# The scores of every attention unit as one float32 product of q and k as loaded, instead of three products of split operands

## The chip, the cores and the metric

The kernel runs on one core of a Trainium2 chip. The metric is the device time of one execution in microseconds (us). Lower is better.

## The reference

Two stages follow each other: an attention with a memory term, and a two-layer network on its output. B, H, S, D are 4, 8, 576, 64.

```python
scores = scale * np.matmul(q, k.transpose(0, 1, 3, 2))
scores = np.where(causal, -1000000000.0, scores)
a = softmax(scores)                       # max subtracted, sum + 1e-09
local = np.matmul(a, v)
q_p = np.where(q > 0, q, np.exp(q) - 1.0) + 1.0
mem_out = einsum(q_p, M_prev) / (einsum(q_p, z_prev)[..., None] + 1e-06)
g = sigmoid(beta)
x = (g * mem_out + (1 - g) * local)       # transposed to 2304 tokens x 512
h = x @ w_in                              # 512 -> 2048
out = (np.maximum(h, 0) ** 2) @ w_out     # 2048 -> 512
```

## The kernel before

The attention is cut into units (b, p, tiles): one batch b, one pair p of heads, and some of the four query tiles 1 to 4 of 128 tokens each (tile 0, the first 64 tokens of all batches, is done at the start by `first_tokens`). Units 0 to 3 are batch 0 with tiles 1 and 2, units 4 to 7 batch 0 with tiles 3 and 4, units 8 to 11 and 12 to 15 the same for batch 1, and units 16 to 23 are batches 2 and 3 with all four tiles. Within a unit the tiles run in the order `TORD` = 2, 1, 3, 4. The keys of tiles 2, 1, 3 are 320, 192, 448 wide, and tile 4 has two groups of 288. The two heads of a pair lie on partitions 0 to 63 and 64 to 127, and their products (`sp`) run beside each other.

A unit does this. `loads` issues, on SyncE's queue (SP), k as `kd`, then q together with the memory as `qm` (of which `q_raw` is the q part), and v as `vv`. `kd` has one buffer (`KB` = 1), `qm` two, `vv` one. The loads of the next unit are issued from `after()`, ahead of the unit's tiles. Of units 6 to 23 (`sfull` false) q and k are split into a high part (`qh`, `kh`, rounded to fp32r on ScalarE) and the rest (`ql`, `kl`, a subtraction on VectorE, in some units GpSimd), and the scores are the sum of three fp32r products. Of units 0 to 5 (`NES` = 6) they are one float32 product of `q_raw` and `kd`. Then come the mask and row maximum (`mx`, VectorE), `e` = exp (ScalarE), the split of e into two f16 halves `a` (L514 on ScalarE, L516 on VectorE), a DMA transpose `aT` on SP's queue, the products with v (`acc`), and the sum with the memory term in `memx`, which goes to DRAM (`xd`) for every two tiles.

The network (`moe`) runs in nine blocks of 256 tokens. A block starts by reading its tokens back (`xn`), transposing them on TensorE (`px`) and splitting them (`xh`, `xl`). Then it has 192 products `up` (L624 to L626) and 96 products `oacc` (L614 to L616). Block 0 is the first tokens, block 1 is batch 0 with tiles 1 and 2 (units 0 to 3), block 2 batch 0 with tiles 3 and 4 (units 4 to 7), and so on. `px` of block 2 therefore needs all of units 4 to 7.

The kernel is written in a framework whose scheduler fixes the order of the instructions on each engine from its own model of the times, and places the waits; each engine then runs its list in order. The names of the steps are those of the code.

Of the kernel before, what the change touches and what calls it, by code (L numbers as in the profile page):

```python
# [8 lines left out]
F32 = mybir.dt.float32  # L9
F32R = mybir.dt.float32r  # L10
# [11 lines left out]
P = 128  # L22
# [6 lines left out]
SQ = S - D  # L29
# [4 lines left out]
SC = 16384.0  # L34
VEXP = 14
VL = 'dd'
PM = 'pd'
FX = 'dd'
GHN = 4
VMIN = 2.0**-80  # L40
NEF = 2
NES = 6
PXT = 'up'
PXE = 'aa'
PHI = 1
QB = 2
VVB = 1
ZW = D + 1
# [2 lines left out]
EB = 3  # L51
# [3 lines left out]
PJ = 6  # L55
SEQ = 'a0 b0 g a1 r b1 r c0 l r r c1'
W0 = 9
EARLY = 'dp'
LATE = 'dd'
NEARLY = 12  # L60
SEG = 2
TORD = [2, 1, 3, 4]
# [25 lines left out]
def fused_kernel(ctx: ExitStack, tc: tile.TileContext, t0_d, zt_d, kk_d, qv_d, beta, w_in, w_out, out):  # L88
    nc = tc.nc
# [3 lines left out]
    at = ctx.enter_context(tc.tile_pool(name="at", bufs=1))  # L93
# [13 lines left out]
        out=mask, in_=mask, pattern=[[-1, MW]], compare_op=ALU.is_ge, fill=-1e30, base=448, channel_multiplier=1  # L107
# [219 lines left out]
    dp = ctx.enter_context(tc.tile_pool(name="dp", bufs=1, space=bass.MemoryType.DRAM))  # L327
# [12 lines left out]
        nc.sync.dma_start(vv[:, :nv], qv_d[b, p, :, SQ + 2 * ZW : SQ + 2 * ZW + nv])  # L340
        return kd, qm, vv

    def attention(b, p, tiles, ld, after, early, sfull, full):
        q_eng, k_eng = (nc.gpsimd if c == 'p' else nc.vector for c in (EARLY if early else LATE))
        late = 0 if early else 1
        h0 = 2 * p
        tl = tiles[-1]
        kn, ncn = sum(QT[tl]), tl + 1
        qa, qb = QT[tiles[0]][0] - D, kn - D
        kd, qm, vv = ld  # L350
        q_raw = qm[:, 2 * ZW :]
        mz = qm[:, : 2 * ZW]
        v = vv.rearrange("p (c x) -> p c x", c=5)
        heads = [slice(h * D, (h + 1) * D) for h in range(2)]

        if not sfull:
            qh, ql = (at.tile([P, SQ], F32R, tag=t, name=t) for t in ("qh", "ql"))
            kh, kl = (at.tile([P, S], F32R, tag=t, name=t) for t in ("kh", "kl"))
            nc.scalar.copy(qh[:, qa:qb], q_raw[:, qa:qb])
            q_eng.tensor_tensor(  # L360
                out=ql[:, qa:qb], in0=q_raw[:, qa:qb], in1=qh[:, qa:qb].bitcast(F32), op=ALU.subtract
            )
            yield
            nc.scalar.copy(kh[:, :kn], kd[:, :kn])
            k_eng.tensor_tensor(out=kl[:, :kn], in0=kd[:, :kn], in1=kh[:, :kn].bitcast(F32), op=ALU.subtract)
            yield
            terms = [(qh, kh), (ql, kh), (qh, kl)]
        else:
            terms = [(q_raw, kd)]

        pe = at.tile([P, 2, S], F32, tag="e", name="pe", bufs=EB)[:, 0]
        w = slice(qa, qb)
        nc.scalar.activation(pe[:, w], q_raw[:, w], AF.Exp)
        ph = pe if sfull else q_raw
        if PHI and not sfull:
            nc.scalar.activation(q_raw[:, w], q_raw[:, w], AF.Relu)
            nc.vector.scalar_tensor_tensor(
                out=q_raw[:, w], in0=pe[:, w], scalar=1.0, in1=q_raw[:, w], op0=ALU.min, op1=ALU.add
            )
        else:  # L380
            m_eng = nc.gpsimd if PM[late] == "p" else nc.vector
            m_eng.tensor_scalar(out=pe[:, w], in0=pe[:, w], scalar1=1.0, scalar2=None, op0=ALU.min)
            nc.vector.scalar_tensor_tensor(
                out=ph[:, w], in0=q_raw[:, w], scalar=0.0, in1=pe[:, w], op0=ALU.max, op1=ALU.add
            )
        yield

        if not full:
# [11 lines left out]
                out=vy, in0=vy, scalar1=VMIN, scalar2=2.0**-VEXP, op0=ALU.max, op1=ALU.mult  # L400
# [19 lines left out]
        for grp in (tiles[:2], tiles[2:]):  # L420
# [4 lines left out]
            for j, i in enumerate(grp):  # L425
# [6 lines left out]
                out=nm[:, :ng], in0=pv[:, :, :, D], scalar=1e-6,  # L432
# [6 lines left out]
                in0=pv[:, :, :, :D],  # L439
# [7 lines left out]
        for i in [t for t in TORD if t in tiles]:  # L447
# [8 lines left out]
            for s in range(ns):  # L456
                ks = slice(s * w, (s + 1) * w)
                sps = ps.tile([P, 2, 512], F32, tag="s", name="sp")
                for x, (qt, kt) in enumerate(terms):
                    for h, hd in enumerate(heads):  # L460
                        nc.tensor.matmul(  # L461
                            sps[:n, h, :w], qt[hd, qc], kt[hd, ks], start=x == 0, stop=x == len(terms) - 1
                        )
                for h in range(2):
                    nc.vector.tensor_tensor_reduce(  # L465
                        out=e[:n, h, ks],
                        in0=sps[:n, h, :w],
                        in1=mask[:n, 448 - q0 + s * w : 448 - q0 + s * w + w],
                        scale=-0.125,
                        scalar=3e38 if s == 0 else mx[:n, h, 0:1],  # L470
                        op0=ALU.add,
                        op1=ALU.min,
                        accum_out=mx[:n, h, s : s + 1],
                    )
# [229 lines left out]
    def attn(i0, i1):  # L704
        for i in range(i0, i1):
            ld = nxt.pop()

            def after():
                if i + 1 < len(order):
                    nxt.append(loads(*order[i + 1]))  # L710

            yield from attention(*order[i], ld, after, i < NEARLY, i < NES, i < NEF and max(order[i][2]) < 4)

    def na(t):
        return NP * (6 + (len(t) > 3) + 2 * len(t) - 1)
# [64 lines left out]
```

## Time and profile before

| what | value |
|---|---|
| median of 3 runs | 610.11 us (610.11 to 610.82) |
| the profiled execution's own time | 609.23 us |
| its span, first to last instruction | 607.4 us |
| TensorE (PE) busy | 569.1 us, 94% of the span |
| VectorE (DVE), ScalarE (ACT), GpSimd (POOL) busy | 411.2, 329.0, 170.3 us |
| mean granted TensorE clock | 0.986 of full speed |

PE is the matmul stream, PEld its weight loads, which overlap it. A line such as L461 is a line of the kernel before. The last scores are computed at about 478 us; after that only the network is left.

### The profile page before, as it was taken

The page shows a single profiled execution, that of the slowest core. Times are in us where ns is not written, and L with a number is a line of the kernel's source. Part 1 is how long each engine was busy: PE and PEld are TensorE (multiplying, and loading weights), DVE is VectorE, ACT ScalarE, POOL GpSimd, SP SyncE. Part 2 cuts the span into 40 slices and gives each one's busy share as a digit, 9 for nine tenths or more (in the row PEclk, how much of TensorE's full clock was granted, in tenths as well). Part 3 has the DMA queues.
Part 4 walks back from the last instruction along what each step waited for, and adds up shares of the span by engine and source line. Part 5 has one row for each costly group of instructions (what it writes and reads, how often), then busy time and mean ns, then how long its engine had stood idle before and what let it go on. Part 6 is the DMA issues. An engine that isn't in the chain of part 4 may idle for free.

```text
span 607.4 us, 11542 instructions
## 1 busy us (share of the span) xinstructions
PE 569.1 (94%) x4198; PEld 482.7 (79%) x4198; DVE 411.2 (68%) x1285; ACT 329.0 (54%) x747; POOL 170.3 (28%) x139
## 2 busy tenths in 40 slices
PE   2479997999989999999999999999999999999997
PEld 2358876787868787888888888888888899998996
DVE  5999798868677879887888978788697711001000
ACT  3689686756566664775576645654556413312312
POOL 2501232134423233233332233232321121221221
PEclk9989998999997999999999999999999999999999
DMA  8947575673574775664655564575435510100000
GB/s 278 402 144 301 165 210 159 139 169 85 117 165 111 160 155 129 145 173 88 164 115 114 145 126 107 114 167 118 103 70 119 99 24 2 68 1 1 36 1 35
DMA packets 127576, 76.28 MB, mean 126 GB/s; under 512 B 99360, under 2 KB 112672, under 8 KB 127520
## 3 DMA queue, kind: packets, MB, share of 16 engines
q1 hardware_dynamic: 127520, 75.55, 49.7%
q8 instruction: 33, 0.54, 0.4%
q14 instruction: 23, 0.19, 0.1%
HBM read 42.63 MB, written 8.78 MB: 85 GB/s over the span
## 4 chain that ended last, share of the span: by engine, by line
PE 63%; DVE 13%; DMA 9%; ACT 9%; issue 3%; SPq 1%; POOL 1%; ACTq 0%
PE up L624 9%; PE up L626 8%; PE up L625 8%; PE oacc L614 8%; PE oacc L616 8%; PE oacc L615 8%; PE sp L461 6%; DMA aT<-a 3%; DMA vv<-in_qv_dram 3%; ACT e L477 2%; PE acc L546 2%; DVE a L516 2%; PE pm L428 2%; DVE e L465 2%; DVE memx L556 2%
## 5 line engine op out<-in xcount | busy, mean ns | idle before, releaser
L624 PE MATMUL up<-xh,w 128*128 128x256 f32 x576 | 167.0, 290 | 3.4 <-ACT aF L496 2.5
L626 PE MATMUL up<-xh,w 128*128 128x256 f32 x576 | 166.1, 288 | 0.0
L625 PE MATMUL up<-xl,w 128*128 128x256 f32 x576 | 165.9, 288 | 0.0
L639 POOL TENSOR_TENSOR gl<-r,gh 128x512 fp32r<-128x512 f32 x72 | 98.9, 1373 | 203.6 <-DVE gh L638 124.4
L624 PEld LDWEIGHTS up<-xh,w 128*128 128x128 f32 x576 | 111.2, 193 | 10.9 <-issue 3.9
L614 PE MATMUL oacc<-w,gh 128*128 128x512 f32 x288 | 116.0, 403 | 3.6 <-ACT gh L636 3.5
L625 PEld LDWEIGHTS up<-xl,w 128*128 128x128 f32 x576 | 111.3, 193 | 5.2 <-issue 2.5
L615 PE MATMUL oacc<-w,gh 128*128 128x512 f32 x288 | 114.4, 397 | 0.0
L626 PEld LDWEIGHTS up<-xh,w 128*128 128x128 f32 x576 | 111.2, 193 | 3.4 <-issue 2.2
L477 ACT ACTIVATE e<-e,mx 128x320 f32<-128x320 f32 (+3 forms) x128 | 77.8, 609 | 65.4 <-DVE mx L465 65.0
L616 PE MATMUL oacc<-w,gl 128*128 128x512 f32 x288 | 111.7, 403 | 0.0
L516 DVE SCALAR_TENSOR_TENSOR a<-e,a 128x128 f16<-128x128 f32 x120 | 79.4, 677 | 19.8 <-ACT a L514 19.6
L630 ACT ACTIVATE r<-up 128x512 f32<-128x512 f32 x72 | 42.4, 590 | 92.5 <-PE up L626 86.6
L632 POOL TENSOR_TENSOR r<-r 128x512 f32<-128x512 f32 x40 | 46.5, 1162 | 164.1 <-ACT r L630 164.1
L638 DVE CAST gh<-r 128x512 fp32r<-128x512 f32 x40 | 16.9, 423 | 87.9 <-ACT r L634 86.4
L614 PEld LDWEIGHTS oacc<-w,gh 128*128 128x128 f32 x288 | 54.5, 189 | 15.7 <-ACT gh L636 4.0
L616 PEld LDWEIGHTS oacc<-w,gl 128*128 128x128 f32 x288 | 53.2, 189 | 13.5 <-issue 3.8
L465 DVE CUSTOM_DVE_ANT_0 e<-sp,mask 128x320 f32<-128x320 f32 (+3 forms) x128 | 56.2, 475 | 9.0 <-PE sp L461 8.9
L615 PEld LDWEIGHTS oacc<-w,gh 128*128 128x128 f32 x288 | 54.5, 189 | 9.4 <-issue 0.9
L514 ACT ACTIVATE a<-e 128x128 f16<-128x128 f32 x120 | 56.9, 521 | 5.7 <-DMA aT<-a 4.7
L548 DVE TENSOR_REDUCE s<-acc 128x128 f32<-128x256 f32 x60 | 24.0, 417 | 21.2 <-PE acc L546 21.2
L546 PE MATMUL acc<-vs,aT 128*128 128x128 f16 x308 | 37.4, 222 | 0.0
(127 smaller groups left out, 883.4 us busy)
## 6 DMA issues: line engine op xcount, KB each, us to landing
raw<-in_w_in_dram SPq DMA_DIRECT2D x11, 512.0 KB, 7.9
vv<-in_qv_dram SPq DMA_DIRECT2D x16, 320.0 KB, 2.8
raw<-in_w_out_dram SPq DMA_DIRECT2D x9, 512.0 KB, 7.8
kd<-in_kk_dram SPq DMA_DIRECT2D x16, 288.0 KB, 3.1
out_dram<-o SPq DMA_DIRECT2D x16, 256.0 KB, 2.0
xd<-memx SPq DMA_DIRECT2D x31, 128.0 KB, 2.1
xn<-xd SPq DMA_DIRECT2D x14, 256.0 KB, 3.2
qm<-in_qv_dram SPq DMA_DIRECT2D x8, 321.0 KB, 2.9
```

Of the source, the lines that this page charges most:

```text
L465: nc.vector.tensor_tensor_reduce(out=e[:n, h, ks], in0=sps[:n, h, :w], in1=mask[:n, 448 - q0 + s * w : 448 - q0 + s * w + w], scale=-0.125 ...
L477: nc.scalar.activation(e[:n, h, :ke], e[:n, h, :ke], AF.Exp, bias=bs, scale=-1.0, accum_out=sm[:n, h : h + 1])
L514: nc.scalar.mul(av[:, :, o0 : o0 + w], x, SC)
L516: nc.vector.scalar_tensor_tensor(out=av[:, :, o0 + w : o0 + 2 * w], in0=x, scalar=SC, in1=av[:, :, o0 : o0 + w], op0=ALU.mult, op1=ALU.sub ...
L546: nc.tensor.matmul(o2, aT[:, h * nb + c, :n], vs[:, h, c], start=False, stop=c == i)
L614: nc.tensor.matmul(acc[t], gh[:, u, ts], w_out_op(f, 0), start=f == 0, stop=False)
L615: nc.tensor.matmul(acc[t], gh[:, u, ts], w_out_op(f, 1), start=False, stop=False)
L616: nc.tensor.matmul(acc[t], gl[:, u, ts], w_out_op(f, 0), start=False, stop=f == NF - 1)
L624: nc.tensor.matmul(up[:, u, :], w_in_op(f, k, 0), xh[:, k, :], start=k == 0, stop=False)
L625: nc.tensor.matmul(up[:, u, :], w_in_op(f, k, 0), xl[:, k, :], start=False, stop=False)
L626: nc.tensor.matmul(up[:, u, :], w_in_op(f, k, 1), xh[:, k, :], start=False, stop=k == NK - 1)
L639: nc.gpsimd.tensor_tensor(out=gl, in0=r, in1=gh.bitcast(F32), op=ALU.subtract)
```

## The change

All units compute their scores as float32 products of `q_raw` and `kd`; `qh`, `ql`, `kh`, `kl` and their four instructions are gone. `q_raw` is no longer overwritten by phi(q): the exponential goes into a tile `ph`, the Relu into a tile `pr` (two buffers each), and ScalarE computes the Relu in all units, so that the GpSimd minimum of units 0 to 5 goes too. The tile `pe`, which took one of the three buffers of `e`, is gone.

```diff
-    def attention(b, p, tiles, ld, after, early, sfull, full):
-        q_eng, k_eng = (nc.gpsimd if c == 'p' else nc.vector for c in (EARLY if early else LATE))
+    def attention(b, p, tiles, ld, after, early, full):
...
-        if not sfull:
-            qh, ql = (at.tile([P, SQ], F32R, tag=t, name=t) for t in ("qh", "ql"))
-            kh, kl = (at.tile([P, S], F32R, tag=t, name=t) for t in ("kh", "kl"))
-            nc.scalar.copy(qh[:, qa:qb], q_raw[:, qa:qb])
-            q_eng.tensor_tensor(
-                out=ql[:, qa:qb], in0=q_raw[:, qa:qb], in1=qh[:, qa:qb].bitcast(F32), op=ALU.subtract
-            )
-            yield
-            nc.scalar.copy(kh[:, :kn], kd[:, :kn])
-            k_eng.tensor_tensor(out=kl[:, :kn], in0=kd[:, :kn], in1=kh[:, :kn].bitcast(F32), op=ALU.subtract)
-            yield
-            terms = [(qh, kh), (ql, kh), (qh, kl)]
-        else:
-            terms = [(q_raw, kd)]
-
-        pe = at.tile([P, 2, S], F32, tag="e", name="pe", bufs=EB)[:, 0]
         w = slice(qa, qb)
-        nc.scalar.activation(pe[:, w], q_raw[:, w], AF.Exp)
-        ph = pe if sfull else q_raw
...
+        ph = at.tile([P, SQ], F32, tag="ph", name="ph", bufs=2)
+        pr = at.tile([P, SQ], F32, tag="pr", name="pr", bufs=2)
+        nc.scalar.activation(ph[:, w], q_raw[:, w], AF.Exp)
+        nc.scalar.activation(pr[:, w], q_raw[:, w], AF.Relu)
+        nc.vector.scalar_tensor_tensor(
+            out=ph[:, w], in0=ph[:, w], scalar=1.0, in1=pr[:, w], op0=ALU.min, op1=ALU.add
+        )
...
-                for x, (qt, kt) in enumerate(terms):
-                    for h, hd in enumerate(heads):
-                        nc.tensor.matmul(
-                            sps[:n, h, :w], qt[hd, qc], kt[hd, ks], start=x == 0, stop=x == len(terms) - 1
-                        )
+                for h, hd in enumerate(heads):
+                    nc.tensor.matmul(sps[:n, h, :w], q_raw[hd, qc], kd[hd, ks], start=True, stop=True)
```

The scheduler orders every engine anew. Two places matter below. The first is on TensorE, where block 2 of the network begins. Before, the transpositions `px` of block 2 are followed by the first score group of unit 10 (`sp`, 320 wide), its memory products `pm` between them, and then block 2's first `up`:

```order
L546 MATMUL acc<-vs,aT 128x128
L591 MATMUL px<-identr,xn 128x128 x8
L397 LDWEIGHTS vx
L397 MATMUL vt<-identb,vx 128x128
L461 MATMUL sp<-kh,qh 128x320 x2
L428 MATMUL pm<-qm 128x130 x2
L461 MATMUL sp<-kh,ql 128x320 x2
L461 MATMUL sp<-kl,qh 128x320 x2
L624 MATMUL up<-xh,w_1007 128x256
```

After the change the 320-wide group of unit 10 stands ahead of `px`, and its 192-wide group is all that stands between `px` and `up`:

```order
L515 MATMUL acc<-vs,aT 128x128
L432 MATMUL sp<-kd,qm 128x320 x2
L560 MATMUL px<-identr,xn 128x128 x8
L432 MATMUL sp<-kd,qm 128x192 x2
L593 MATMUL up<-xh,w_1011 128x256
L594 MATMUL up<-xl,w_1011 128x256
L595 MATMUL up<-xh,w_1011 128x256
```

So `px` moved behind one more group of scores, and the group behind it got smaller. In the listing before, 37 `up` and 36 `oacc` stand between the last scores of unit 7 and these `px`; after the change 4 `up` and 24 `oacc` do, since the scores of units 5 to 7 stand later among block 1's products.

The second place is SP's queue at the same point: `xd` is what unit 7 writes, `xn` what block 2 reads back, and the last `kd` ahead of `xn` is that of unit 9 before and of unit 10 after. Before:

```order
L520 DMA_TRANSPOSE aT<-a 128x10x128
L567 DMA xd_91<-memx 128x2x128
L333 DMA kd<-in_kk_dram 128x320
L520 DMA_TRANSPOSE aT<-a 128x6x128
L340 DMA vv<-in_qv_dram 128x384
L337 DMA qm<-in_qv_dram 128x386
L588 DMA xn<-xd_91 128x512 x2
```

After the change:

```order
L328 DMA kd<-in_kk_dram 128x320
L489 DMA_TRANSPOSE aT<-a 128x10x128
L489 DMA_TRANSPOSE aT<-a 128x6x128
L536 DMA xd_91<-memx 128x2x128
L332 DMA qm<-in_qv_dram 128x386
L328 DMA kd<-in_kk_dram 128x320
L557 DMA xn<-xd_91 128x512 x2
```

The `kd` load now stands directly ahead of `xn`, and it waits for the last score product that reads the buffer's old contents.

## Rows read from the trace of the kernel before

**Rows 1.** The page's first part: busy time of each engine, its share of the span, and its instructions.

```profile
PE 569.1 (94%) x4198; PEld 482.7 (79%) x4198; DVE 411.2 (68%) x1285; ACT 329.0 (54%) x747; POOL 170.3 (28%) x139
```

**Rows 2.** Busy time by stretch of the span: length, then busy time (and instructions) of PE, PEld, DVE, ACT, POOL, the granted clock, the DMA share, GB/s.

```profile
0.00:110.00 110.00, 82.22 (x563) 66.58 (x563) 96.63 (x275) 76.53 (x179) 27.74 (x28) 0.95 0.72 234
181.00:189.00 8.00, 7.77 (x40) 6.64 (x40) 6.50 (x28) 4.35 (x14) 0.00 (x0) 0.57 0.45 107
189.00:480.00 291.00, 288.96 (x2259) 241.93 (x2259) 237.83 (x767) 170.56 (x397) 89.83 (x70) 1.00 0.57 125
```

**Rows 3.** Who PE waited for: total us, times, the longest.

```profile
PE sp L461 <- DVE mx L465: 6.4, 5, 4.3
PE oacc L614 <- ACT gh L636: 3.5, 1, 3.5
PE acc L541 <- DMA aT<-a: 1.9, 2, 1.0
```

**Rows 4.** Groups of instructions by line, of the whole span: count, busy us and mean ns, idle time of the engine before them. The first four are the splits; the last is the Relu.

```profile
L359 ACT CAST qh<-qm 128x256 fp32r<-128x256 f32 (+1 forms) x18 | 8.9, 496 | 0.6 <-DMA qm<-in_qv_dram 0.6
L364 ACT CAST kh<-kd 128x576 fp32r<-128x576 f32 (+1 forms) x18 | 11.2, 622 | 28.2 <-PE sp L461 28.2
L360 DVE TENSOR_TENSOR ql<-qm,qh 128x256 fp32r<-128x256 f32 (+1 forms) x18 | 13.2, 733 | 0.4 <-ACT qh L359 0.3
L365 DVE TENSOR_TENSOR kl<-kd,kh 128x576 fp32r<-128x576 f32 x12 | 9.0, 750 | 0.0
L376 ACT ACTIVATE qm<-qm 128x256 f32<-128x256 f32 (+1 forms) x18 | 9.0, 503 | 0.2 <-DVE ql L360 0.2
```

**Rows 5.** The products of one of the three terms of units 6 to 23, by width (two heads, so half of each count is the number of groups).

```profile
L461 PE MATMUL sp<-kh,qh x132: 353/398/632, 131.3 to 477.3; 64*128 64x288 f32 x56, 64*128 64x448 f32 x28, 64*128 64x320 f32 x24, 64*128 64x192 f32 x24
```

**Rows 6.** PE in order of time (start us, duration, what), at four score groups of units 0 to 5 (one float32 product for each head, two instructions each), each with the instruction that starts next: 320, 192, 448 and 288 wide.

```profile
72.14 0.81 PE L461 MATMUL sp<-kd,qm 64*128 64x320 f32 x4
72.88 0.39 PE L624 MATMUL up<-xh,w 128*128 128x256 f32 x1
...
77.50 0.60 PE L461 MATMUL sp<-kd,qm 64*128 64x192 f32 x4
78.03 0.50 PE L616 MATMUL oacc<-w,gl 128*128 128x512 f32 x1
...
113.28 1.02 PE L461 MATMUL sp<-kd,qm 64*128 64x448 f32 x4
114.24 0.39 PE L624 MATMUL up<-xh,w 128*128 128x256 f32 x1
...
117.96 0.76 PE L461 MATMUL sp<-kd,qm 64*128 64x288 f32 x4
118.64 0.39 PE L625 MATMUL up<-xl,w 128*128 128x256 f32 x1
```

**Rows 7.** The same of split units: a 320-wide group that is broken in two, with products of the network between (first nine rows), and the first instruction and the next stranger of unbroken groups of 288, 192 and 448.

```profile
272.14 0.40 PE L616 MATMUL oacc<-w,gl 128*128 128x512 f32 x1
272.47 0.41 PE L461 MATMUL sp<-kh,qh 64*128 64x320 f32 x2
272.81 0.50 PE L614 MATMUL oacc<-w,gh 128*128 128x512 f32 x1
273.15 0.40 PE L615 MATMUL oacc<-w,gh 128*128 128x512 f32 x1
273.38 0.39 PE L616 MATMUL oacc<-w,gl 128*128 128x512 f32 x1
...
274.42 0.28 PE L625 MATMUL up<-xl,w 128*128 128x256 f32 x1
274.53 0.28 PE L626 MATMUL up<-xh,w 128*128 128x256 f32 x1
...
275.46 0.41 PE L461 MATMUL sp<-kh,ql 64*128 64x320 f32 x2
...
275.95 0.38 PE L624 MATMUL up<-xh,w 128*128 128x256 f32 x1
...
289.32 0.40 PE L461 MATMUL sp<-kh,qh 64*128 64x288 f32 x2
...
289.92 0.50 PE L615 MATMUL oacc<-w,gh 128*128 128x512 f32 x1
...
304.82 0.36 PE L461 MATMUL sp<-kh,qh 64*128 64x192 f32 x2
...
305.33 0.50 PE L615 MATMUL oacc<-w,gh 128*128 128x512 f32 x1
...
307.39 0.47 PE L461 MATMUL sp<-kh,qh 64*128 64x448 f32 x2
...
308.19 0.39 PE L626 MATMUL up<-xh,w 128*128 128x256 f32 x1
```

**Rows 8.** All 24 `kd` loads: us from the issue to the landing.

```profile
DMA to landing us min/median/max: 2.2/3.0/9.3
```

**Rows 9.** PE in order of time: the last scores of unit 7, the `px` of block 2, and block 2's first `up`.

```profile
158.24 0.52 PE L461 MATMUL sp<-kl,qh 64*128 64x288 f32 x2
...
180.80 1.35 PE L591 MATMUL px<-identr,xn 128*128 128x128 f32 x8 [2.10 <-DMA xn<-xd]
...
184.96 0.55 PE L624 MATMUL up<-xh,w 128*128 128x256 f32 x1
```

More of the change, by code (lines that the diff above doesn't have):

```diff
@@ L36 @@
 VL = 'dd'
-PM = 'pd'
 FX = 'dd'
@@ L41 @@
 NEF = 2
-NES = 6
 PXT = 'up'
 PXE = 'aa'
-PHI = 1
 QB = 2
@@ L57 @@
 W0 = 9
-EARLY = 'dp'
-LATE = 'dd'
 NEARLY = 12
@@ L354, in attention @@
         heads = [slice(h * D, (h + 1) * D) for h in range(2)]
-        if not sfull:
-            qh, ql = (at.tile([P, SQ], F32R, tag=t, name=t) for t in ("qh", "ql"))
-            kh, kl = (at.tile([P, S], F32R, tag=t, name=t) for t in ("kh", "kl"))
-            nc.scalar.copy(qh[:, qa:qb], q_raw[:, qa:qb])
-            q_eng.tensor_tensor(
-                out=ql[:, qa:qb], in0=q_raw[:, qa:qb], in1=qh[:, qa:qb].bitcast(F32), op=ALU.subtract
-            )
-            yield
-            nc.scalar.copy(kh[:, :kn], kd[:, :kn])
-            k_eng.tensor_tensor(out=kl[:, :kn], in0=kd[:, :kn], in1=kh[:, :kn].bitcast(F32), op=ALU.subtract)
-            yield
-            terms = [(qh, kh), (ql, kh), (qh, kl)]
-        else:
-            terms = [(q_raw, kd)]
-        pe = at.tile([P, 2, S], F32, tag="e", name="pe", bufs=EB)[:, 0]
-        w = slice(qa, qb)
-        nc.scalar.activation(pe[:, w], q_raw[:, w], AF.Exp)
-        ph = pe if sfull else q_raw
[L375 to L378, printed above, removed]
-            )
[L380 to L385, printed above, removed]
+        w = slice(qa, qb)
+        ph = at.tile([P, SQ], F32, tag="ph", name="ph", bufs=2)
[5 more added lines that the diff above has]
+        )
         yield
@@ L458, in attention @@
                 sps = ps.tile([P, 2, 512], F32, tag="s", name="sp")
-                for x, (qt, kt) in enumerate(terms):
-                    for h, hd in enumerate(heads):
-                        nc.tensor.matmul(
-                            sps[:n, h, :w], qt[hd, qc], kt[hd, ks], start=x == 0, stop=x == len(terms) - 1
-                        )
+                for h, hd in enumerate(heads):
+                    nc.tensor.matmul(sps[:n, h, :w], q_raw[hd, qc], kd[hd, ks], start=True, stop=True)
                 for h in range(2):
@@ L710, in after @@
                     nxt.append(loads(*order[i + 1]))
-            yield from attention(*order[i], ld, after, i < NEARLY, i < NES, i < NEF and max(order[i][2]) < 4)
+            yield from attention(*order[i], ld, after, i < NEARLY, i < NEF and max(order[i][2]) < 4)
     def na(t):
```

## The prediction

> **What bounds the kernel now.** I read the busy times first. TensorE is busy for 94% of the span and no other engine for more than 68% [rows 1]. That average covers two stages, so the second view is the busy time by stretch [rows 2]. In the first 110 us VectorE is the full engine (96.63 us) and TensorE has 82.22. From 189 to 480 us, where nearly all the split units lie, TensorE is busy for 288.96 of 291.00 us. So whatever the other engines save there can give back at most 2.04 us by shorter waits; the rest of the effect must come from TensorE's own products, or from waits that the change creates.
>
> The third view is who TensorE waited for [rows 3]: `mx` 6.4 us in five waits, 4.3 of it in one that lies in the first 110 us; `gh` 3.5 us in one, also early; `aT` 1.9 in two. The remaining one that matters is where block 2 begins: `px` waited 2.10 us for `xn` [rows 9], and behind it the granted clock is 0.57 of full speed over 181 to 189 us [rows 2], that is, mostly at the 1.2 GHz level after the engine had stood still.
>
> **Splits removed.** ScalarE loses 8.9 + 11.2 = 20.1 us, VectorE 13.2 + 9.0 = 22.2 us [rows 4], GpSimd some `kl` more. I cost this at nothing by itself: it lies beside a TensorE that is full. If that cover were gone, one unit's chain would be 0.50 + 0.73 or 0.62 + 0.75 us shorter [rows 4], about 1.3 us, which I use below. ScalarE gets a Relu in six more units, 6 x 0.50 = 3.0 us [rows 4], in the stage that VectorE fills; nothing, and 3.0 at worst.
>
> **A. Score products, -2.6 us.** Here both forms stand in the trace. From a group's start to the next instruction's start, the float32 product takes 0.53 us at 192 columns, 0.68 at 288, 0.74 at 320, 0.95 to 0.96 at 448 [rows 6] (78.03 - 77.50 = 0.53, and so on). The three products, unbroken, take 0.51, 0.60 and 0.80 at 192, 288, 448 [rows 7]; between 288 and 448 that makes 0.64 at 320. By width the new form is dearer. Units 6 to 23 have 28 groups of 288, 14 of 448, 12 each of 320 and 192 (half the counts in [rows 5]): three products 28 x 0.60 + 14 x 0.80 + 12 x 0.64 + 12 x 0.51 = 41.8 us, float32 47.6 us, so +5.8.
>
> But many groups of three are broken: products of the network stand between their terms. The 320-wide one in [rows 7] takes 272.81 - 272.47 = 0.34 and 275.95 - 275.46 = 0.49. Entering it took 0.33 from the `oacc` before, where `oacc` after `oacc` takes 0.23 (273.38 - 273.15), and leaving it 0.34 where 0.23 is usual: 0.21 more. Broken, it costs 0.34 + 0.49 + 0.21 = 1.04, which is 0.40 over 0.64. In the order before, 21 of the 66 groups are broken in two (11 of 320, 5 of 448, 4 of 288, 1 of 192); in the order of the change none is. 21 x 0.40 = 8.4, and 5.8 - 8.4 = -2.6. Bounds: +5.8 if breaks cost nothing, -4 if the longer break of other groups costs a little more.
>
> A rule of the Trainium skill speaks against this term: FP8 and Floating Point Precision, section TensorE Precision Notes, has "True FP32: 4 passes through PE array". Read as four passes in place of three products, that is a third more at every width, 41.8 x 4/3 = 55.7, and the term would be +13.9 - 8.4 = +5.5. The rows agree with it only in part: 19% more at 448 columns, 4% at 192. I go by the rows.
>
> **B. Ahead of block 2's `px`, +4.4 us.** `px` needs all of units 4 to 7. From the last scores of unit 7 to `px` it took 180.80 - 158.24 = 22.6 us [rows 9]: mask and maximum, exp, halves, transposes, products with v, `memx`, its way to DRAM and back. TensorE filled that time with 37 `up` and 36 `oacc`, at 0.12 (274.53 - 274.42) and 0.23 us [rows 7] 4.4 + 8.3 = 12.7 us, and with scores, memory terms and products with v of other units; still it stood 2.10 us. In the changed order 4 `up` and 24 `oacc` are left in between, 6.0 us. I take the chain 1.5 us shorter, about one unit's splits, 21 us. What that work doesn't cover is 21 - 6.0 = 15.0 against 22.6 - 12.7 = 9.9, so 5.1 more; of that the 320-wide group that now stands ahead fills 0.74. Bounds: nothing, if the chain without its queueing behind products is 17 us or less; +7, if the `kd` load that now stands directly ahead of `xn` on SP's queue lands late (its median is 3.0, its worst 9.3 us [rows 8], and 2 us of that more than my 21).
>
> **C. From `px` to block 2's first `up`, +1.5 us.** That took 184.96 - 180.80 = 4.16 us, of which `px` itself 1.35 [rows 9]; meanwhile VectorE and ScalarE make `xh` and `xl`. The rest, 2.8, was filled by the broken 320-wide group and `pm`. Now only a 192-wide group stands there, 0.53 [rows 6]. So 0 (if `xh` is quick) to 2.3; I take 1.5, nearer the top, since [rows 9] don't show how long `xh` had been ready when the `up` came.
>
> **D. Small waits after 110 us, -2.5 us.** `mx` without its long wait is 2.1 us, `aT` 1.9 [rows 3], together 4.0; both come behind the engines that lose the splits. I take somewhat over half; bounds 0 and -4.0.
>
> **E. Clock behind the longer gap, +0.8.** 8 us at 0.57 lost 3.4 us [rows 2]; a gap three times as long could keep the low level for half as long again, 1.7, or leave it as it is. The middle.
>
> **F. The early wait for `gh`, -1.0.** 3.5 us once [rows 3]; the order there changes, since products with v move in front of it. Bounds 0 and -3.5; it needs VectorE and ScalarE, which are as full there as before, so less than a third.
>
> **G. `kd` held longer, +0.5.** There is one buffer. In split units it was free once `kh` and `kl` were made; now the last score product of the unit frees it. In the changed order, 4.4 to 6.7 us of TensorE work (by the durations above) stand between that product and the next unit's first. A load lands 3.0 us after issue in the median [rows 8], so it fits by 1.4 us at the tightest place, and a bad one, 9.3, doesn't. Behind a late `kd` wait, on SP's queue, `aT`, `xd` and `xn`. Bounds 0 and +17 (below).
>
> **The sum.** -2.6 + 4.4 + 1.5 - 2.5 + 0.8 - 1.0 + 0.5 = +1.1. The profiled execution took 609.23 us, of which 607.4 is the span; 609.2 + 1.1 = 610.3. The median of the runs is 0.9 us above the profiled time, so I expect **611.2 us**.
>
> **Rivals.** *Faster: no wider gap.* If the chain ahead of `px` is no more than 17 us, or mostly queueing behind TensorE's own products, B, C, E and G vanish and A, D, F stay: -2.6 - 2.5 - 1.0 = -6.1, that is 603.1 and, with the 0.9, 604.0 (607.5 if only A holds). For it: VectorE and ScalarE have over 40 us less to do, so the chain of unit 7 queues less. Against it: 2.10 us of waiting even with 12.7 us of cover. It decides at a chain of 17 us.
>
> *Slower: `kd` late at every unit.* If the load lands 5.4 us after the last score product rather than 3.0 (because it stands behind a waiting transfer on SP's queue), the tightest units lose 1.0 us and 17 of them up to 17: 624 to 628. Against it: the fit above, by 1.4 us or more.
>
> *Slower: the float32 product at four thirds of the three.* The three products unbroken are 41.8 us; a third more is 55.7, so A becomes 13.9 - 8.4 = +5.5 and the time 619.3. For it, the growth with the width: from 192 to 448 columns the float32 product grows by 0.43 us, the three by 0.29 [rows 6, 7]. Against it: the times of whole groups in [rows 6], measured in this kernel. The rule of the Trainium skill quoted under A is what this rival would confirm.
>
> *The change does nothing that shows.* The breaks' cost in A is overstated by half, and the network's products simply close up around what is saved: 610 +- 1.
>
> **How the numbers follow.** A measurement of this kernel tells about 0.2% (1.2 us) from no change, so faster is below 608.9, slower above 611.3. Forecast, a wider gap that the cheaper scores and lost waits about pay for: 0.46, own range 608 to 615, of which faster 0.06, same 0.18, slower 0.22. No wider gap: 0.32, faster. Nothing that shows: 0.09, same. `kd` late everywhere: 0.08, and four thirds 0.05, slower. Together 0.38, 0.27, 0.35. For 8 in 10 the range leaves out the lowest part of the second case (D and F near their bounds), the `kd` rival and half of the four thirds: 602 to 618.
>
> **What would show it.** A: float32 groups of units 6 to 23 at the times of [rows 6] and never broken; 1 us or more off at 448 shows it wrong. B: TensorE's wait for `xn` ahead of block 2 at 5 to 9 us rather than 2.1. C: a wait at the first `up` behind it. D, F: no waits of 0.4 us or more for `mx` and `aT` after 110 us, and a shorter one for `gh`. E: a granted clock under 0.6 for longer than 8 us there. G: `sp` never waiting for `kd` by more than 0.5 us in sum. The prediction is wrong if the gap at `px` stays at 2 us (then I am too high by some 6) or if `sp` waits for `kd` again and again (too low).

## The result and the profile after

| | before | after |
|---|---|---|
| median | 610.47 us (4 runs, 610.11 to 610.91) | 616.96 us (4 runs, 614.83 to 619.68) |
| the profiled execution: time, span | 609.23, 607.4 us | 619.68, 617.9 us |
| mean granted TensorE clock of it | 0.986 | 0.972 |

The change makes the kernel slower: ratio 1.0108, 95% interval 1.0067 to 1.015. The forecast was 611.2 us with a range of 602 to 618, so the time lies in the range but 5.8 us above the point. The profiled execution is the longest of the four. The other three took 616.55, 617.37 and 614.83 us at clocks of 0.977, 0.977 and 0.981, so the spread of the changed kernel goes with its clock. Of the experiments below, e10 had its one traced execution at a mean clock of 0.849, against 0.978 to 0.985 in its other three; that trace is left out, and the median of e10 is that of the three.

The busy times of the page of after answer to [rows 1]. VectorE and ScalarE lost 20.7 and 11.9 us of work, GpSimd 17.4, and TensorE is still the full engine:

```profile
PE 573.2 (93%) x4066; PEld 476.7 (77%) x4066; DVE 390.5 (63%) x1255; ACT 317.1 (51%) x717; POOL 152.9 (25%) x127
```

The stretches of [rows 2] for after, and two more stretches of 110 to 480 us, first of before and then of after (length, busy time and instructions of PE, PEld, DVE, ACT, POOL, granted clock, DMA share, GB/s):

```profile
0.00:110.00 110.00, 82.95 (x558) 66.40 (x558) 96.78 (x270) 79.42 (x184) 21.53 (x22) 0.94 0.67 228
181.00:189.00 8.00, 4.70 (x34) 2.95 (x32) 6.71 (x32) 5.50 (x18) 0.00 (x0) 0.71 0.83 207
189.00:480.00 291.00, 283.79 (x2109) 230.66 (x2110) 219.69 (x752) 157.17 (x369) 81.88 (x67) 0.98 0.59 125
```

```profile
110.00:480.00 370.00, 363.11 (x2821) 303.87 (x2822) 299.56 (x976) 219.67 (x514) 115.38 (x90) 0.99 0.58 127
```

```profile
110.00:480.00 370.00, 356.00 (x2632) 288.69 (x2631) 276.04 (x942) 201.49 (x472) 100.60 (x82) 0.97 0.59 127
```

TensorE stands 370 - 356.00 = 14.0 us between 110 and 480 us, where it stood 6.9 before. In the first 110 us it stands 27.05 instead of 27.78. So 6.4 of the 10.5 us between the two profiled spans are standing.

Where it lies is seen by cutting the span behind the low clock that follows block 2's `px`, at 195 us; first two stretches of before, then the same two of after (columns as above):

```profile
115.00:195.00 80.00, 75.39 (x587) 63.05 (x587) 60.76 (x204) 48.76 (x121) 28.62 (x23) 0.96 0.60 131
195.00:480.00 285.00, 282.96 (x2203) 236.82 (x2203) 233.99 (x756) 165.98 (x384) 86.76 (x68) 1.00 0.57 126
```

```profile
115.00:195.00 80.00, 73.01 (x531) 58.42 (x529) 56.94 (x195) 44.88 (x109) 18.73 (x15) 0.94 0.56 125
195.00:480.00 285.00, 277.99 (x2075) 225.34 (x2074) 214.60 (x729) 153.05 (x356) 81.88 (x67) 0.99 0.60 127
```

TensorE stands 6.99 us instead of 4.61 up to 195 us, and 7.01 instead of 2.04 behind it. So 5.0 of the 6.4 us of standing lie behind the place where block 2 begins.

The rest is a balance of two terms. A mean clock of 0.972 over 617.9 us costs 0.028 x 617.9 = 17.3 us against a span at 2.4 GHz throughout; before it was 0.014 x 607.4 = 8.5. That is up to 8.8 us more, a little less where the low level met an idle engine. What is left, 10.5 - 6.4 - 8.8, is about -4.7, or a little less: the products themselves got cheaper.

Who TensorE waited for, against [rows 3] (us in total, times, longest):

```profile
PE sp L432 <- DVE mx L434: 11.8, 8, 4.8
...
PE acc L510 <- DMA aT<-a: 5.9, 3, 3.1
...
PE acc L510 <- DVE vs L382: 2.4, 2, 1.3
PE px L560 <- DMA xn<-xd: 1.9, 2, 1.2
...
PE sp L432 <- DMA kd<-in_kk_dram: 1.4, 1, 1.4
...
PE oacc L583 <- ACT gh L605: 1.2, 1, 1.2
```

The long waits for `mx` and `aT` did not go: `mx` without its longest is 7.0 us (2.1 before), `aT` 5.9 (1.9 before). Only `gh` fell, from 3.5 to 1.2.

The score groups of split units, now float32, each with the instruction that starts next (448, 288, 320 and 192 wide), answer to [rows 6] and [rows 7]:

```profile
209.76 1.02 PE L432 MATMUL sp<-kd,qm 64*128 64x448 f32 x4
210.72 0.39 PE L593 MATMUL up<-xh,w 128*128 128x256 f32 x1
...
214.82 0.76 PE L432 MATMUL sp<-kd,qm 64*128 64x288 f32 x4
215.50 0.50 PE L585 MATMUL oacc<-w,gl 128*128 128x512 f32 x1
...
278.97 0.81 PE L432 MATMUL sp<-kd,qm 64*128 64x320 f32 x4
279.71 0.73 PE L585 MATMUL oacc<-w,gl 128*128 128x512 f32 x2
...
284.11 0.59 PE L432 MATMUL sp<-kd,qm 64*128 64x192 f32 x4
284.64 0.73 PE L585 MATMUL oacc<-w,gl 128*128 128x512 f32 x2
```

0.96, 0.68, 0.74 and 0.53 us: the durations that the early units had shown, to 0.01 us.

Where the standing around block 2 begins is seen in TensorE's own order of time (start, duration, what, and in brackets the idle time and its releaser). The stretch runs from the last scores of unit 7 (164.95) to the `px` of block 2 (186.88) and its neighbour, and answers to [rows 9]:

```profile
164.95 0.76 PE L432 MATMUL sp<-kd,qm 64*128 64x288 f32 x4
...
173.82 0.60 PE L432 MATMUL sp<-kd,qm 64*128 64x192 f32 x4 [0.29 <-DVE mx L434]
177.56 0.23 PE L510 MATMUL acc<-vs,aT 128*128 128x128 f16 x1 [3.15 <-DMA aT<-a]
...
178.64 1.44 PE L432 MATMUL sp<-kd,qm 64*128 64x320 f32 x4
180.01 1.24 PE L400 MATMUL pm<-qm,ph 128*128 128x130 f32 x4
...
183.26 0.22 PE L510 MATMUL acc<-vs,aT 128*128 128x128 f16 x1 [1.07 <-DVE vs L382]
...
185.51 1.44 PE L432 MATMUL sp<-kd,qm 64*128 64x320 f32 x4 [1.36 <-DMA kd<-in_kk_dram]
186.88 1.26 PE L560 MATMUL px<-identr,xn 128*128 128x128 f32 x8
189.20 1.01 PE L432 MATMUL sp<-kd,qm 64*128 64x192 f32 x4 [1.06 <-DVE mx L434]
```

From the last scores of unit 7 to `px` it is 21.9 us, and TensorE stands 0.29 + 3.15 + 1.07 + 1.36 = 5.87 of them. `px` itself no longer waits: the chain of unit 7 is about as long as before, but with fewer products to fill it TensorE comes too early inside it and not at its end, 3.15 us for unit 7's own transposed halves `aT`, then for `vs` of unit 8 and `kd` of unit 10. Behind the waits the same 320-wide group that takes 0.74 us elsewhere takes 180.01 - 178.64 = 1.37: the lower clock (0.66 over 178 to 193 us, below).

### The profile page after: what moved, and what is told of

The parts are those of the page before. It is cut to its first block, busy times and chain, and to the rows that moved or that the text cites. A ratio compares the mean times of both kernels' runs of the same rounds, so it can differ in the third digit from the quotient of the medians.

```text
span 617.9 us, 11127 instructions
## 1 busy us (share of the span) xinstructions
PE 573.2 (93%) x4066; PEld 476.7 (77%) x4066; DVE 390.5 (63%) x1255; ACT 317.1 (51%) x717; POOL 152.9 (25%) x127
## 4 chain that ended last, share of the span: by engine, by line
PE 71%; DMA 12%; DVE 11%; issue 2%; SPq 2%; ACT 1%; ACTq 0%
PE up L593 10%; PE up L594 10%; PE up L595 10%; PE oacc L583 9%; PE oacc L585 9%; PE oacc L584 8%; PE sp L432 7%; DMA vv<-in_qv_dram 4%; DMA aT<-a 3%; PE acc L515 2%; PE pm L400 2%; DVE a L485 1%; DVE e L434 1%; PE acc L504 1%; DVE w L161 1%
## 5 line engine op out<-in xcount | busy, mean ns | idle before, releaser
L593 PE MATMUL up<-xh,w 128*128 128x256 f32 x576 | 169.7, 295 | 0.0
L594 PE MATMUL up<-xl,w 128*128 128x256 f32 x576 | 168.6, 293 | 0.0
L595 PE MATMUL up<-xh,w 128*128 128x256 f32 x576 | 167.5, 291 | 0.0
L608 POOL TENSOR_TENSOR gl<-r,gh 128x512 fp32r<-128x512 f32 x72 | 95.9, 1332 | 239.6 <-DVE gh L607 126.3
L593 PEld LDWEIGHTS up<-xh,w 128*128 128x128 f32 x576 | 113.8, 198 | 10.3 <-issue 6.5
L594 PEld LDWEIGHTS up<-xl,w 128*128 128x128 f32 x576 | 113.8, 198 | 5.6 <-issue 3.2
L595 PEld LDWEIGHTS up<-xh,w 128*128 128x128 f32 x576 | 113.8, 198 | 2.8 <-issue 2.0
L599 ACT ACTIVATE r<-up 128x512 f32<-128x512 f32 x72 | 42.5, 590 | 100.1 <-PE up L595 95.9
L485 DVE SCALAR_TENSOR_TENSOR a<-e,a 128x128 f16<-128x128 f32 x120 | 72.6, 615 | 26.9 <-ACT a L483 26.5
L432 PE MATMUL sp<-kd,qm 64*128 64x288 f32 (+3 forms) x320 | 68.1, 494 | 18.4 <-DVE mx L434 11.8
L432 PEld LDWEIGHTS sp<-kd,qm 64*128 64x128 f32 x320 | 26.1, 195 | 35.3 <-DVE mx L434 15.2
```

Source lines behind the costliest of these rows:

```text
L432: nc.tensor.matmul(sps[:n, h, :w], q_raw[hd, qc], kd[hd, ks], start=True, stop=True)
L485: nc.vector.scalar_tensor_tensor(out=av[:, :, o0 + w : o0 + 2 * w], in0=x, scalar=SC, in1=av[:, :, o0 : o0 + w], op0=ALU.mult, op1=ALU.sub ...
L593: nc.tensor.matmul(up[:, u, :], w_in_op(f, k, 0), xh[:, k, :], start=k == 0, stop=False)
L594: nc.tensor.matmul(up[:, u, :], w_in_op(f, k, 0), xl[:, k, :], start=False, stop=False)
L595: nc.tensor.matmul(up[:, u, :], w_in_op(f, k, 1), xh[:, k, :], start=False, stop=k == NK - 1)
L608: nc.gpsimd.tensor_tensor(out=gl, in0=r, in1=gh.bitcast(F32), op=ALU.subtract)
```

## The experiments

What is common to them, first. The scheduler orders every kernel anew, so I counted in each order how many products of the network stand between the last scores of unit 7 and the `px` of block 2 ("cover"), and read in each trace how long TensorE stood in that stretch, ahead of `px`, and how long the eight `px` then waited for `xn`. "Standing" is TensorE's idle time up to 480 us, "clock" is (1 - mean granted clock) x span, both of the profiled execution; "rest" is its time less both.

| kernel | median us | ratio to before (95%) | cover: up, oacc | stood there | at `px` | standing | clock | profiled time | rest |
|---|---|---|---|---|---|---|---|---|---|
| before | 610.5 | | 37, 36 | 0.45 | 2.10 | 34.7 | 8.5 | 609.2 | 566 |
| after | 617.0 | 1.0108 (1.0067 to 1.0150) | 1, 24 | 5.87 | 0 | 41.1 | 17.3 | 619.7 | 561 |
| e1 kd2 | 617.4 | 1.0112 (1.0057 to 1.0166) | 48, 35 | 0 | 0.82 | 41.5 | 11.7 | 617.7 | 564 |
| e2 vv2 | 610.2 | 0.9987 (0.9959 to 1.0016) | 62, 35 | 0 | 0 | 39.0 | 9.1 | 610.6 | 562 |
| e3 kd2 and vv2 | 617.5 | 1.0127 (1.0068 to 1.0185) | 38, 36 | 0 | 2.62 | 39.0 | 13.5 | 615.5 | 563 |
| e4 float32, old phi | 611.6 | 1.0008 (0.9983 to 1.0033) | 24, 33 | 0.22 | 3.75 | 35.6 | 8.5 | 608.8 | 565 |
| e5 ph in e | 616.2 | 1.0097 (1.0062 to 1.0133) | 39, 36 | 0.60 | 1.73 | 42.5 | 8.6 | 616.2 | 565 |
| e6 no Relu | 611.9 | 1.0033 (1.0009 to 1.0057) | 38, 36 | 1.45 | 2.08 | 40.1 | 12.2 | 614.0 | 562 |
| e7 Relu first | 618.2 | 1.0124 (1.0086 to 1.0162) | 1, 24 | 5.46 | 0 | 41.5 | 15.4 | 617.9 | 561 |
| e8 new phi alone | 618.4 | 1.0124 (1.0044 to 1.0203) | 3, 24 | 5.01 | 1.36 | 39.9 | 16.0 | 616.9 | 561 |
| e9 Relu from unit 6 | 607.1 | 0.9953 (0.9929 to 0.9977) | 24, 34 | 1.07 | 2.10 | 33.0 | 12.1 | 607.9 | 563 |
| e10 Relu to unit 5 | 617.0 | 1.0118 (1.0066 to 1.0170) | 8, 24 | | | | | | |
| e11 float32, old phi, vv2 | 614.6 | 1.0073 (1.0044 to 1.0103) | 78, 36 | 0 | 0 | 43.0 | 10.4 | 616.1 | 563 |
| e12 before, vv2 | 605.8 | 0.9934 (0.9912 to 0.9956) | 69, 31 | 0 | 0 | 35.8 | 9.1 | 607.0 | 562 |

The last column carries the first reading. Over all these kernels, with three products or one, the rest stays within 561 to 566 us, while the profiled time moves by 13. What differs is how long TensorE stands and how long it runs at the lower clock behind that.

### Does the loss come from the single buffer of k, or of v?

e1 and e2 edit the changed kernel; e3 has both edits.

```diff
-KB = 1
+KB = 2
```

> The changed kernel with two buffers for kd instead of one, nothing else edited (the scheduler orders anew). Theory L (loads): the loss of 6.5 us comes from the kd load that waits for the last score product of a unit, and from what queues behind it on SP (aT, xd, xn). Then score products never wait for kd (1.36 us before), TensorE's idle time after 110 us falls from 14.0 to 8 us or less, the time at the lower clock falls with it, and the median is 609 to 612. Theory O (order): the loss comes from where the scheduler now places scores, transposes and products with v among the network's products, whatever the buffer. Then only the 1.4 us goes and the median is 614 to 619.

```diff
-VVB = 1
+VVB = 2
```

> The changed kernel with two buffers for vv instead of one. In its trace VectorE stands 2.15 us at vx for the vv load (to 318.87 us), and 3 us later score products wait 2.32 us for the mx that stands behind it in VectorE's queue; the same again at 424 us (0.71, then 1.24). Theory V: these waits come from vv's single buffer. Then both waits are gone, and the clock's drop at 325 us too: 612 to 614. Theory O: waits of the same sum turn up elsewhere, 615 to 619.

> The changed kernel with two buffers for kd and for vv. If the loads are the cause (L and V), the gains of the two add: 606 to 610, under the kernel before. If the order is (O), 614 to 619.

e1 came out at 617.4: with two buffers score products no longer wait for `kd`, and nothing is won. Behind 110 us TensorE stands 370 - 360.40 = 9.6 us, 4.4 less than in after, which is most of what theory L asked for; but in the first 110 us it stands 110 - 78.07 = 31.9, 4.9 more. As an account of the loss, theory L falls. e2 came out at 610.2, as fast as the kernel before, which looks like theory V. But e3, which contains it, is at 617.5, so gains do not add, and a second buffer of v is not enough by itself. The chain behind V's wait is plain in the trace of after, on VectorE, TensorE and SP:

```profile
318.87 0.82 DVE L365 TENSOR_REDUCE vx<-vv 128x1 f32<-128x640 f32 x1 [2.15 <-DMA vv<-in_qv_dram]
...
320.90 2.21 DVE L485 SCALAR_TENSOR_TENSOR a<-e,a 128x128 f16<-128x128 f32 x2
323.04 0.68 DVE L566 TENSOR_TENSOR xl<-px,xh 128x512 fp32r<-128x512 f32 x1
323.64 0.44 DVE L434 CUSTOM_DVE_ANT_0 e<-sp,mask 128x288 f32<-128x288 f32 x1
```

```profile
318.67 0.76 PE L432 MATMUL sp<-kd,qm 64*128 64x288 f32 x4
...
324.52 0.76 PE L432 MATMUL sp<-kd,qm 64*128 64x288 f32 x4 [2.32 <-DVE mx L434]
```

```profile
315.79 0.53 SPq L335 DMA_DIRECT2D vv<-in_qv_dram  x1
```

VectorE has the next unit's `vx` ahead of this unit's `mx` in its queue; `vx` waits 2.15 us for a load that was issued at 315.79, and the `mx` for scores that were done at 319.43 runs only at 323.64. In e2 TensorE waits 2.20 us for `mx` from 291.64 instead. So there the wait moved and did not go, although the kernel got faster by 7 us.

### Which half of the change loses the time?

e4 is the kernel before with `NES = 24`: float32 scores and no splits, but phi(q) made the old way.

```diff
-NES = 6
+NES = 24
```

> The kernel before with all 24 units of the kind of its first six: float32 scores of q and k as loaded, but phi(q) made as those units made it (into a tile that takes one of e's three buffers, with a minimum on GpSimd or VectorE and no Relu on ScalarE). It is the change without its second half. If the float32 scores and the lost splits make the loss, it is 614 to 620 as after the change. If the new tiles for phi(q) and the free third buffer of e make the new order worse, it is 608 to 612. If they help, it is over 622, since phi now competes for e's buffers in every unit.

It came out at 611.6, ratio 1.0008. With one buffer of v, the half that the title of the change names costs nothing and wins nothing that can be measured. (With two buffers of v the same edit costs almost 9 us: e12, at the end of this section, took 605.8 and e11 614.6. So this is a statement on two orders, not on the price of float32 scores.) The loss of the change then hangs on the other half, on how phi(q) is made. Four kernels take that apart. e5 puts `ph` back into e's buffers, e6 drops the Relu, e7 exchanges the two ScalarE lines, e8 is the new phi beside three split products:

```diff
-        ph = at.tile([P, SQ], F32, tag="ph", name="ph", bufs=2)
+        ph = at.tile([P, 2, S], F32, tag="e", name="ph", bufs=EB)[:, 0]
```

> The changed kernel with one edit: ph takes one of e's three buffers again, as pe did, instead of two of its own. Theory E: the loss against the kernel with float32 scores and the old phi (611.6) comes from the third buffer of e, which lets scores run further ahead of the work behind them. Then this gives it back: 609 to 613. Theory R (the Relu on ScalarE and its tile are the cause): it stays at 615 to 620. Theory P (any small edit makes the scheduler set another order, and orders differ by some us through which waits they leave): anything from 608 to 620, with the waits after 110 us at new places, and no relation to what was edited.

```diff
-        nc.scalar.activation(pr[:, w], q_raw[:, w], AF.Relu)
-        nc.vector.scalar_tensor_tensor(
-            out=ph[:, w], in0=ph[:, w], scalar=1.0, in1=pr[:, w], op0=ALU.min, op1=ALU.add
-        )
+        m_eng.tensor_scalar(out=ph[:, w], in0=ph[:, w], scalar1=1.0, scalar2=None, op0=ALU.min)
+        nc.vector.scalar_tensor_tensor(
+            out=ph[:, w], in0=q_raw[:, w], scalar=0.0, in1=ph[:, w], op0=ALU.max, op1=ALU.add
+        )
```

> The changed kernel without the Relu: phi(q) by the old two steps (minimum of the exponential on GpSimd for units 0 to 11 and on VectorE for the rest, then maximum and sum on VectorE), in the new tile ph. Theory R: 609 to 613, as with the old phi. Theory E: 615 to 620, since e keeps its three buffers. Theory P: anything from 608 to 620.

```diff
-        nc.scalar.activation(ph[:, w], q_raw[:, w], AF.Exp)
         nc.scalar.activation(pr[:, w], q_raw[:, w], AF.Relu)
+        nc.scalar.activation(ph[:, w], q_raw[:, w], AF.Exp)
```

> The changed kernel with the Relu written ahead of the exponential: the same instructions, tiles and buffers, only two independent lines of ScalarE exchanged. Theories E and R: no change, 614 to 620, within 2 us of the changed kernel. Theory P: the order comes out anew and the time moves by 2 to 8 us, most likely down, since the changed kernel is among the slow ones so far.

```diff
# the kernel before, with
-        pe = at.tile([P, 2, S], F32, tag="e", name="pe", bufs=EB)[:, 0]
+        ph = at.tile([P, SQ], F32, tag="ph", name="ph", bufs=1)
+        pr = at.tile([P, SQ], F32, tag="pr", name="pr", bufs=1)
...
```

> The second half of the change alone: scores of three products with the splits as before, but phi(q) made in ph and pr (one buffer each, as two do not fit beside the splits) with the Relu in all units. Theories E and R: this half carries the loss, 614 to 619. Theory P: anything from 606 to 618. If the two halves only lose together, 609 to 612.

e5 keeps the loss (616.2), e6 is back near the kernel before (611.9, ratio 1.0033), e7 is as slow as the change (618.2), and e8, which has no float32 scores beyond those of before, has the loss too (618.4, though its four runs spread from 612.5 to 621.2). Theory E falls by e5. Theory P, that any edit moves the time by several us, did not hold for e7: its order has the same 1 `up` and 24 `oacc` in the stretch, and its waits stand where those of after stand:

```profile
175.95 0.29 PE L510 MATMUL acc<-vs,aT 128*128 128x128 f16 x1 [3.18 <-DMA aT<-a]
...
182.06 0.22 PE L510 MATMUL acc<-vs,aT 128*128 128x128 f16 x1 [1.35 <-DVE vs L382]
```

e8 shows that float32 scores are not needed for it. With three products, TensorE stands at the same step of the same stretch:

```profile
163.48 0.40 PE L454 MATMUL sp<-kh,qh 64*128 64x288 f32 x2
...
176.44 0.23 PE L534 MATMUL acc<-vs,aT 128*128 128x128 f16 x1 [1.98 <-DMA aT<-a]
```

So among these kernels, with one buffer of v, the Relu in all units goes with the loss, but hardly by its own time: in units 6 to 23 ScalarE computed it before as well, at 0.50 us [rows 4], with another engine bound. With two buffers of v it does not go with it: e2 has the Relu in all units and takes 610.2, e11 has it in none and takes 614.6. What after, e7 and e8 share is an uncovered stretch ahead of block 2. e5 does not share it: its stretch is covered, and it stands 291 - 279.03 = 12.0 us behind 189 us.

### Is it the stretch ahead of block 2?

e9 and e10 split the Relu by units. e9 leaves it where the kernel before had it.

```diff
+        if not first6:
             pr = at.tile([P, SQ], F32, tag="pr", name="pr", bufs=2)
             nc.scalar.activation(pr[:, w], q_raw[:, w], AF.Relu)
...
+        else:
+            m_eng.tensor_scalar(out=ph[:, w], in0=ph[:, w], scalar1=1.0, scalar2=None, op0=ALU.min)
...
```

> The changed kernel with the Relu only in units 6 to 23, where the kernel before had it as well; units 0 to 5 take the minimum instead. So far the orders with the Relu in all units that left 1 to 3 up and 24 oacc between the last scores of unit 7 and px of block 2 stood 5.0 to 5.9 us in that stretch and were slow; the others have 24 to 62 up and 33 to 36 oacc there and stood 0 to 1.5 us. This one's order has 24 up and 34 oacc. Theory G (the gap ahead of block 2, filled or not, decides): 610 to 613, with less than 2 us of standing in that stretch ahead of the wait for xn. Theory R (the Relu itself, wherever it is): 615 to 619.

e10 is its complement, with the condition turned round.

> The complement: the Relu only in units 0 to 5, the minimum in units 6 to 23. Its order has 8 up and 24 oacc in the stretch named. Theory G: 3.5 to 5 us of standing there, lower clock behind it, 614 to 618. Theory R with the cost in the later units: 610 to 613.

e9 came out at 607.1, faster than both kernels compared so far and 3 us below what theory G gave it, and e10 at 617.0. The whole loss of the change, and more, hangs on the Relu of the six early units. In e9 the last scores of unit 7 stand 5.8 us earlier than in after, and the products that this frees lie in the stretch:

```profile
159.19 0.76 PE L439 MATMUL sp<-kd,qm 64*128 64x288 f32 x4
...
171.68 0.23 PE L517 MATMUL acc<-vs,aT 128*128 128x128 f16 x1 [1.07 <-DMA aT<-a]
...
180.38 0.75 PE L567 MATMUL px<-identr,xn 128*128 128x128 f32 x4 [2.10 <-DMA xn<-xd]
```

From its last scores to `px` it is 21.2 us here and 21.9 in after: the chain is about the same, the cover is not. But e9's order is another one behind block 2 as well. TensorE stands 80 - 76.76 = 3.24 us over 115 to 195 us, against 6.99 in after, and 285 - 282.13 = 2.87 over 195 to 480, against 7.01. So only about half of the standing that e9 saves lies near this stretch, and e9 does not single it out as the cause.

### Does cover there give speed in general?

e11 is e4 with two buffers of v, e12 the kernel before with two buffers of v.

> Float32 scores with the old phi and two buffers for vv: the parts of the change without its Relu, with the one edit that helped. Its order has 78 up and 36 oacc in the stretch named. Theory G: no standing there, no lower clock behind px of block 2, 605 to 609, less than both kernels. If two buffers of vv helped only by the order that they gave by chance, 609 to 615.

> The kernel before with two buffers for vv and nothing else. Its order has 69 up and 31 oacc in the stretch named, against 37 and 36. Theory G: the 2.10 us ahead of px and the 3.4 us of lower clock behind it go, 605 to 608. If vv's buffer mattered only where the splits are gone: 609 to 612.

e12 came out at 605.8, ratio 0.9934: the fastest of all, and the split kernel at that. It does not stand in the stretch, nor at `px`, and its clock over 181 to 189 us is 1.00 where [rows 2] have 0.57:

```profile
181.00:189.00 8.00, 7.58 (x56) 6.26 (x57) 7.97 (x29) 4.39 (x13) 1.62 (x2) 1.00 0.51 108
```

e11 is a miss. It has the most cover and stands 0 us in the stretch, but it took 614.6 instead of 605 to 609. It stands elsewhere: 3.73 us for `xn` at block 1's `px` (114.09), and 3.6 us in three waits for `kd`, which still has one buffer. Two of these:

```profile
205.37 1.02 PE L461 MATMUL sp<-kd,qm 64*128 64x448 f32 x4 [1.26 <-DMA kd<-in_kk_dram]
...
381.60 0.81 PE L461 MATMUL sp<-kd,qm 64*128 64x320 f32 x4 [1.93 <-DMA kd<-in_kk_dram]
```

```profile
377.32 0.42 SPq L333 DMA_DIRECT2D kd<-in_kk_dram  x1
```

The load for the scores at 381.60 was issued at 377.32, behind `xd` and `xn` on SP's queue. So cover ahead of block 2 is not enough: e1, e3, e5 and e11 have it, stand at other places and are slow.

Nor is it as sharp as the column "stood there" makes it, since that leaves out the wait at `px`. e4, with 24 `up` and 33 `oacc`, waits there longer than any other kernel:

```profile
178.57 0.75 PE L591 MATMUL px<-identr,xn 128*128 128x128 f32 x4 [3.75 <-DMA xn<-xd]
```

Both columns together are 3.97 us in e4 and 3.17 in e9, which are not slow, and 5.87, 5.46 and 6.37 in after, e7 and e8, which are. That is 1.5 to 3.2 us apart. The lower clock behind the waits adds to it: over 115 to 195 us, standing and (1 - mean granted clock) x 80 us together make 7 us in e4 and 6 in e9, 12 in after, 14 in e7 and 17 in e8. So what happens around block 2's `px` gives less than half of the 11 to 12 us by which the profiled execution of after is longer than those of e4 and e9, but most of the 9 to 10 of e7 and all of the 8 to 9 of e8. Theory G agrees in direction with after, e7, e8, e9, e10 and e12; it does not rank all kernels.

## Why the prediction was right or wrong

**A, the products: right in price.** The four widths cost what [rows 6] said, and of units 6 to 23 the trace of after has no broken group. The sum was put at -2.6; the balance above leaves -4.7, but the split kernels e8 and e12 have as small a rest, so the size of this term is known to a few us only. The rival "four thirds" (+5.5) is out, and with it the four passes of the Trainium skill (FP8 and Floating Point Precision, TensorE Precision Notes) read as a price: 0.96 against 0.80 us at 448 columns is 20% more, 0.53 against 0.51 at 192 is 4%.

**B, the gap ahead of block 2: right in mechanism, nearly in size, wrong in place.** The chain was put at 21 us and is 21.9; in the other orders it is 20.7 to 24.9. TensorE stands 5.87 us in the stretch, against 0.45 + 2.10 before: +3.3 where the term says +4.4. But the wait for `xn` that I named as its sign is not there. I had taken the chain as one wait at its end; TensorE works through the chain's own products and those of units 8 to 10 in between, and stands at each for which it comes too early. The count that the term rests on was three too high (1 `up`, not 4).

**C: a misreading.** I took the `up` behind `px` for block 2's first, which needs `xh`. It is block 1's. A block has 64 products of line L624, and before `px` at 180.80 there had been 120 of them, 64 + 56:

```profile
L624 PE MATMUL up<-xh,w x120: 274/283/415, 39.3 to 167.6; 128*128 128x256 f32 x120
```

`prefetch` is called with an eighth of the block still to come, so nothing waits for `xh` there. The 1.06 us that stand in after at 189.20 are for `mx`, which the term did not name. Its +1.5 was near that by luck.

**D, small waits after 110 us: wrong in sign.** The step that failed is "both come behind the engines that lose the splits". Behind 189 us TensorE stands 291 - 283.79 = 7.21 us instead of 2.04: +5.2 where I put most of a -2.5. VectorE and ScalarE do have less to do, but a shorter queue does not help an instruction that stands in the wrong place of it. The `mx` at 323.64 waits behind another unit's `vx`; the `acc` at 231.78 waits 1.93 us for an `aT` that went out on SP's queue at 225.46, behind loads, and landed 6.3 us later, where 4.0 is the median. The bound of 0 for this term assumed that waits could only go, although the scheduler was known to order anew; it needed a bound on the side of loss.

**E, the clock: much too small.** I put +0.8 for one gap. The mean clock says 17.3 us against 8.5, up to +8.8. Only about 1.6 of that lies around block 2's `px` (0.94 instead of 0.96 over 80 us), where the term had it; about 2.9 lie behind 195 us (0.99 instead of 1.00 over 285), after the waits at 231.78 and 324.52, and about 3.4 in the first 115 us (0.93 instead of 0.96), where TensorE is not the full engine.

**F: right.** `gh` fell by 2.3 us, other waits took some of it, and the first 110 us stand 0.7 us less (I put -1.0).

**G, `kd`: right in size.** One wait of 1.36 us (+0.5), and e1, which removes it, wins nothing.

**Sum and sides.** Standing +6.4, clock +8.8, products -4.7 make the 10.5 us of the profiled executions. The medians differ by 6.5, as the profiled execution of after lies 2.7 us above its median and that of before 1.2 below. That the time lies inside the range is in part luck: the case forecast had 608 to 615, and the range went on to 618 for half of the four thirds, which did not come. I had given 0.35 to slower. The step that decided it was one that I costed at nothing, "ScalarE gets a Relu in six more units": e9, without those six, is 9.9 us faster than the change (9.5 by the two ratios). That is more than the 3.0 us of ScalarE that I bounded them by, so the rest comes with the order that goes with them.

**What stays open.** Why the Relu of six early units makes the scheduler set unit 7's scores 5 to 6 us later is in the scheduler's own model of times; no run looks into it. Nor was an order held fixed while one price was changed, so "the order does it" is argued, not shown: it rests on after, e7, e8 and e10 against e4, e6 and e9, and on the waits seen in the traces. How much of the loss the stretch ahead of block 2 makes, and how much the waits behind 195 us, no run separates. A rival that stays is the load of v: in after VectorE waits 20.1 us in 17 waits for `vv`, 13.4 in 10 before, and one of 1.63 us (`vx` at 169.09) stands just ahead of the last halves of unit 7. A second buffer of v made the change and the kernel before faster (e2, e12), but not e1 (e3) and not e4 (e11).

## What to carry to other kernels

When a scheduler orders the program, an edit has two prices: that of its instructions, and that of the new order. Here the first was about -5 us and the second, in the medians, about +11, and single edits beside the change (six Relus, a second buffer for v) moved the time by 4 to 10 us. So compare the new order with the old. One thing to count: between a chain's first product and its last on the full engine, how much work that doesn't depend on it stands in between, against the length of the chain in the trace (21 us here, with 12.7 us of cover before and 5.6 after). Here that would have shown one of the losses of the change and not the larger part, which came elsewhere; and a part of a change that costs nothing in one order (float32 scores, e4) can go with almost 9 us in another (e11 against e12), so one comparison does not price it. And give an edit that "lies beside the full engine" a bound on the side of loss, as it moves what the full engine waits for.

## What the runs showed of the hardware that was not expected

A wait of TensorE costs more than itself, but not always. In after the clock was 0.66 over a stretch that follows the wait of 3.15 us and holds those of 1.07, 1.36 and 1.06, and 0.81 over two stretches that hold one wait of 1.93 and one of 2.32 us (columns as above):

```profile
178.00:193.00 15.00, 11.45 (x73) 8.20 (x70) 11.94 (x51) 9.26 (x29) 0.00 (x0) 0.66 0.73 170
229.00:238.00 9.00, 7.07 (x54) 5.75 (x51) 4.91 (x16) 3.30 (x8) 1.46 (x2) 0.81 0.48 108
321.00:330.00 9.00, 6.68 (x51) 5.88 (x51) 7.66 (x22) 3.38 (x7) 1.30 (x1) 0.81 0.57 135
```

In e5 two waits of 1.92 and 1.95 us were followed by no lower clock at all:

```profile
213.00:222.00 9.00, 6.99 (x54) 5.77 (x52) 6.25 (x20) 3.12 (x7) 2.31 (x2) 1.00 0.49 102
223.00:232.00 9.00, 7.05 (x50) 5.46 (x49) 6.36 (x23) 6.41 (x14) 2.31 (x2) 1.00 0.72 174
```

So the same standing of about 2 us came out with 1.7 us on top (19% of 9 us) or with none, which may also be how one kernel's runs differ by 5 us (after: clocks of 0.972 to 0.981, times of 619.7 to 614.8).
